# State products of two steps in 64 by 64 tiles, with the second step's heads swapped between the row halves

## The chip, the cores and the metric

The kernel runs on one core of one Trainium2 chip. The metric is device time in microseconds (us) of that core, the median of five runs. Engines are named as in the profile: PE (TensorE), PEld (its weight loads), DVE (VectorE), ACT (ScalarE), POOL (GpSimd), SP (the queue that issues most of the DMAs).

## The reference, cut to what matters

Decaying linear attention over 4 batches, 8 heads of 64 and 768 positions is followed by a feed-forward block with a sine gate.

```python
for b in range(nb):                                   # blocks of 64 positions
    intra = np.einsum('bhic,bhjc->bhij', qb, kb) * Dmask[None]
    intra = np.einsum('bhij,bhjd->bhid', intra, vb)
    inter = np.einsum('bhid,bhde->bhie', qb * lam_pow[None], kv_state)
    out[:, :, sl] = intra + inter
    kv_state = lam_block * kv_state + np.einsum('bhsd,bhse->bhde', kb * rev_pow, vb)
x = attn_out.transpose(0, 2, 1, 3).reshape(B * S, H * D)
h = x @ w_in                                          # 3072 x 512 @ 512 x 2048
s = np.sin(alpha * h)
g = h + s * s / (alpha + 1e-09)
out = g @ w_out                                       # 3072 x 2048 @ 2048 x 512
```

## The kernel before, in words

The 3072 rows are taken in 24 *steps* of 128 positions; a step is one block of 128 positions of one batch with its 8 heads. Steps come in pairs: an even and an odd step are the same block of two batches (`place`), so each batch has its own state and a pair shares nothing but buffers. Blocks are 128 long here (the reference's 64 are regrouped), and q and k are scaled by powers of lambda beforehand, so that the state is a plain running sum. Four steps make a *chunk* of 512 rows, and six chunks go through the feed-forward block.

Of one step s the orders name these pieces; the letter is the tag in the written orders, and the line that of the profile:

- `Lk`, `Lq`, `Lv`: loads, issued by SP (L392).
- `k`, `q`, `v`: scaling to bf16 (L507; L513 for the first 8 steps, L516 for the others) and the cast of v (L471), on POOL, DVE or ACT.
- `T` (L536, L539), for steps 0 to 7: 8 transposes of 128x128 by PE into a bank of PSUM and a copy `tc`; later steps are transposed by a DMA (`DT`, SP). The result is qkT: rows 0-63 hold the even head of each head pair, rows 64-127 the odd head.
- `S` (L554): scores of 8 heads, 8 matmuls that contract over 64 rows, give 128 keys x 128 queries, and go to two banks, one for each row half. `mask` (L559): two DVE products of 128x512.
- `P` (L570): product of q with the state, 4 matmuls of 128 rows x 128 columns. The state Zs is held as blocks of 128x128, one for each head pair, with zeros off the diagonal, so one matmul does both heads. P opens the bank (start).
- `I` (L577): masked scores times v, 8 matmuls of 128 rows and 64 output partitions, added to the same bank; then `x` (L471) copies the bank to xT.
- `Z` (L599), once per pair: 16 matmuls of 64 columns that add k'v to the state of both steps in the bank Z_ps; then `zs` (L471): two copies of 64x512, one per half of the rows, into Zs. The zeros are written once at the start (L454).
- The first block of a batch has no P; the last has no Z.

Of one chunk: `A` (L619), 16 products of 4 matmuls of 512 columns; `sin` (ACT, L624), `sq` (L629 on ACT, L630 on POOL or DVE), `g` (DVE, L632); `B` (L642), for each of its 4 steps 16 matmuls of 512 columns in four parts `B chunk.step.part`; `oc` copies it out (L471) and `st` stores it (L653). The very last step has its own function, `half_tile`: two groups `H0`, `H1` (L663) of 256 columns each, with copies `hc` and stores `hs`. `warm` (L676) are matmuls on zeros, in five groups of 14, 5, 2, 2 and 7 that fill PE before the first A.

Everything runs in an order that is written out by hand for each engine: the table `ORDER` (L19 to L85) has one list of tags for PE, DVE, ACT, POOL and SP. Semaphore waits are derived from what each piece reads and writes. `c0`, `c1`, ... are the constants in the order in which they are recorded; in PE's list, `c28` is the transpose of alpha (L463), which waits for alpha's DMA and is PE's first instruction. Seven banks `m_ps` go round by a list of free banks that follows PE's order. The weights come in 13 blocks `Lw` through a staging buffer, each cast in pieces `wc` by POOL, DVE or ACT.

Two stretches of PE's list, the start and the attention of steps 8 to 11, in chunk 1's output products:

```python
"c28 warm0 T1 T0 warm1 S1 warm2 S0 warm3 T3 T2 I1 S3 I0 Z0 S2 warm4 P3 P2 I3 I2 Z1 A0.2 A0.1 A0.0 "
...
"A1.13 A1.15 A1.8 A1.11 B1.1.0 B1.3.0 B1.3.1 B1.0.0 B1.1.1 B1.0.1 S8 S9 B1.1.2 B1.0.2 B1.0.3 P9 P8 I9 "
"I8 Z4 S11 S10 B1.3.2 B1.2.0 B1.3.3 P10 P11 I10 I11 B1.1.3 A2.9 A2.2 A2.4 A2.14 A2.1 A2.3 A2.13 "
```

Of the kernel before, what the change touches and what calls it, by code (L numbers as in the profile page):

```python
# [5 lines left out]
ALU = mybir.AluOpType  # L6
# [7 lines left out]
CHUNKS = [(0, 4), (4, 4), (8, 4), (12, 4), (16, 4), (20, 4)]  # L14
NG, NW, NPQ = 2, 6, 8
WARM = (
    14, 5, 2, 2, 7,
# [3 lines left out]
        "c28 warm0 T1 T0 warm1 S1 warm2 S0 warm3 T3 T2 I1 S3 I0 Z0 S2 warm4 P3 P2 I3 I2 Z1 A0.2 A0.1 A0.0 "  # L21
        "A0.7 A0.6 A0.4 A0.5 A0.3 A0.11 A0.8 A0.9 A0.10 A0.15 A0.14 A0.13 B0.1.0 A0.12 B0.0.0 B0.0.1 B0.3.0 "
        "B0.1.1 B0.3.1 B0.3.2 T4 B0.1.2 B0.2.0 B0.0.2 T5 S4 B0.0.3 B0.3.3 S5 P5 T6 B0.1.3 P4 T7 I4 S6 B0.2.1 "
        "Z2 I5 S7 B0.2.2 P6 P7 Z3 I6 I7 B0.2.3 A1.6 A1.10 A1.7 A1.5 A1.0 A1.9 A1.3 A1.1 A1.4 A1.2 A1.12 A1.14 "
        "A1.13 A1.15 A1.8 A1.11 B1.1.0 B1.3.0 B1.3.1 B1.0.0 B1.1.1 B1.0.1 S8 S9 B1.1.2 B1.0.2 B1.0.3 P9 P8 I9 "
        "I8 Z4 S11 S10 B1.3.2 B1.2.0 B1.3.3 P10 P11 I10 I11 B1.1.3 A2.9 A2.2 A2.4 A2.14 A2.1 A2.3 A2.13 "
        "B1.2.1 A2.12 A2.8 A2.7 A2.5 A2.10 A2.0 A2.6 B1.2.2 A2.11 B1.2.3 A2.15 B2.1.0 B2.1.1 S12 S13 B2.1.2 "
        "B2.2.0 B2.2.1 B2.1.3 B2.2.2 I13 Z6 I12 S15 S14 B2.3.0 B2.3.1 P14 B2.3.2 P15 I15 I14 Z7 S17 B2.2.3 "
        "A3.1 A3.0 B2.3.3 A3.10 A3.14 A3.2 A3.3 A3.13 B2.0.0 B2.0.1 A3.6 A3.12 A3.7 A3.8 A3.4 A3.5 B2.0.2 "
        "B2.0.3 A3.15 A3.9 A3.11 B3.0.0 B3.0.1 B3.3.0 B3.3.1 P17 I17 Z8 S16 S19 B3.3.2 B3.3.3 P16 I16 S18 "  # L30
        "B3.0.2 B3.0.3 P18 P19 I19 I18 Z9 B3.2.0 A4.0 A4.3 A4.5 A4.6 A4.10 A4.2 A4.4 A4.11 A4.14 B3.2.1 A4.7 "
        "A4.1 B3.2.2 B3.2.3 A4.15 A4.8 B3.1.0 B3.1.1 A4.13 A4.9 A4.12 B4.2.0 B3.1.2 B4.3.0 B4.3.1 B3.1.3 S20 "
        "S21 B4.2.1 B4.3.2 B4.3.3 P21 P20 Z10 I20 I21 S23 S22 B4.2.2 B4.2.3 B4.0.0 P23 P22 I22 I23 B4.0.1 "
        "A5.1 B4.0.2 A5.2 A5.7 A5.8 A5.6 B4.1.0 B4.0.3 B4.1.1 A5.0 A5.3 A5.12 A5.10 A5.4 A5.5 B4.1.2 A5.11 "
        "A5.9 B4.1.3 B5.1.0 A5.15 B5.2.0 A5.14 B5.2.1 A5.13 B5.1.1 B5.0.0 B5.0.1 B5.0.2 B5.1.2 B5.0.3 B5.1.3 "
        "B5.2.2 B5.2.3 H1 H0 "
    ),
    "DVE": (
        "c10 c11 c19 c25 c12 c3 c14 c15 c5 c16 c1 k0 k3 tc1 mask1.1 mask1.0 mask0.0 mask0.1 tc2 mask3.1 "
        "mask3.0 mask2.0 mask2.1 x0 x2 wc1.0 c31 wc1.6 sq0.1 g0.1 g0.2 g0.0 sq0.7 sq0.4 sq0.6 g0.7 g0.6 g0.4 "  # L40
        "g0.5 g0.3 g0.11 sq0.8 g0.8 g0.9 sq0.10 g0.10 wc2.10 g0.15 wc2.8 g0.14 q5 g0.13 g0.12 wc2.14 mask4.1 "
        "mask4.0 k7 mask5.0 mask5.1 tc6 oc1 tc7 mask6.0 mask6.1 mask7.1 mask7.0 x6 oc2 q9 q8 sq1.6 g1.6 "
        "sq1.10 g1.7 g1.10 sq1.9 zs3.1 g1.5 g1.0 g1.9 g1.3 g1.1 g1.4 sq1.2 g1.2 g1.12 sq1.14 g1.14 g1.13 "
        "g1.15 g1.11 g1.8 v8 mask8.0 mask9.0 mask8.1 mask9.1 q15 x8 mask11.0 mask10.1 mask11.1 mask10.0 x10 "
        "v13 oc7 sq2.9 k12 g2.9 g2.2 sq2.4 g2.14 g2.4 sq2.3 g2.1 g2.3 sq2.12 g2.13 g2.12 sq2.5 g2.8 g2.5 g2.7 "
        "g2.0 g2.6 g2.11 g2.10 oc6 mask12.0 v16 g2.15 mask13.1 v12 mask13.0 mask12.1 oc9 mask15.1 mask14.0 "
        "mask15.0 mask14.1 x15 v18 q19 mask17.0 oc10 q18 sq3.1 mask17.1 sq3.0 g3.0 g3.1 oc11 sq3.10 g3.14 "
        "g3.10 g3.2 g3.3 sq3.6 g3.13 g3.12 g3.6 g3.8 g3.7 g3.5 g3.4 sq3.15 g3.15 v19 oc8 g3.9 g3.11 mask16.0 "
        "mask16.1 mask19.1 zs8.1 mask18.0 mask19.0 mask18.1 q23 x19 oc12 g4.0 g4.3 g4.5 sq4.6 g4.10 g4.6 "
        "zs9.1 g4.4 g4.2 sq4.11 g4.11 g4.14 g4.1 oc14 g4.7 g4.8 g4.15 g4.13 g4.9 g4.12 mask21.1 mask20.0 "  # L50
        "mask21.0 mask20.1 x20 mask23.0 mask22.0 mask22.1 mask23.1 x22 g5.1 g5.2 sq5.6 oc16 g5.8 g5.7 g5.6 "
        "g5.3 g5.0 sq5.12 g5.12 g5.10 g5.4 g5.5 g5.9 g5.11 g5.14 g5.13 g5.15 oc22 hc1 "
    ),
    "ACT": (
        "lam c27 c0 c4 c17 c7 c29 c6 c18 tc0 c26 tc3 wc1.2 x1 zs0.0 zs0.1 v2 x3 sin0.2 sin0.1 sin0.0 sq0.2 "
        "sin0.7 sin0.6 sin0.4 wc1.8 sin0.5 sin0.3 sin0.11 sq0.3 sq0.11 sin0.8 sin0.9 wc2.2 sq0.9 sin0.10 "
        "wc2.6 sin0.15 sq0.15 sin0.13 sin0.14 sin0.12 sq0.14 zs1.1 sq0.12 tc4 wc2.12 tc5 zs1.0 oc0 oc3 v4 v5 "
        "x4 zs2.0 zs2.1 x5 x7 zs3.0 sin1.6 sin1.10 sin1.7 sq1.7 st0 sin1.5 sin1.9 sin1.0 sin1.3 sin1.1 sin1.4 "
        "sq1.4 sin1.12 sin1.2 sin1.13 sin1.15 sin1.14 sq1.15 sq1.13 sin1.11 v11 sin1.8 sq1.8 oc4 x9 zs4.1 "
        "zs4.0 st3 x11 oc5 st2 sin2.9 sin2.2 sq2.2 sin2.14 sin2.4 sq2.14 sin2.1 sin2.3 sq2.1 sin2.13 sin2.12 "  # L60
        "sq2.13 sin2.8 sin2.5 sin2.7 sq2.8 sin2.0 sin2.6 sin2.10 sin2.11 sq2.11 sq2.10 v15 sin2.15 sq2.15 x13 "
        "zs6.0 x12 zs6.1 st6 x14 zs7.0 sin3.1 sin3.0 sin3.10 sin3.14 sin3.2 sq3.2 sq3.14 sin3.13 sin3.3 "
        "sq3.13 sin3.6 sin3.12 st4 sin3.7 sin3.8 sin3.4 sq3.7 sin3.5 sq3.5 zs7.1 sin3.15 sin3.9 sin3.11 sq3.9 "
        "sq3.11 x17 x16 zs8.0 oc15 v23 x18 sin4.0 sin4.3 sin4.5 zs9.0 sq4.3 sin4.10 sin4.6 sq4.10 sin4.2 "
        "sin4.4 sq4.2 sin4.14 sin4.7 sin4.11 sin4.1 sq4.7 sq4.1 sin4.15 sin4.8 v20 sq4.8 sq4.15 sin4.13 "
        "sq4.13 st14 sin4.9 sin4.12 sq4.9 oc13 oc19 zs10.1 x21 zs10.0 oc18 x23 sin5.1 sq5.1 sin5.2 sin5.7 "
        "sin5.8 sin5.6 sq5.7 sq5.8 sin5.0 sin5.3 sq5.3 sq5.0 sin5.10 sin5.4 sin5.12 sq5.10 sin5.5 sq5.4 "
        "sin5.9 sin5.11 sq5.11 oc17 sin5.14 sq5.14 sin5.13 sin5.15 sq5.13 oc20 oc21 st21 hc0 hs0 "
    ),
    "POOL": (  # L70
        "c8 c23 c9 c20 c22 c13 c2 k1 q0 q2 c24 q1 k2 q3 c30 v1 v0 v3 wc1.4 sq0.0 wc1.10 wc1.14 sq0.5 wc1.12 "
        "wc2.0 q4 wc2.4 sq0.13 k4 k5 q6 k6 q7 v7 v6 k8 k9 sq1.5 sq1.0 sq1.3 sq1.1 q10 sq1.12 k10 k11 q11 "
        "sq1.11 v10 v9 c21 q12 k13 v17 q14 q13 k14 q17 sq2.7 sq2.0 sq2.6 k15 v14 k17 k16 k19 k18 q21 sq3.3 "
        "k21 sq3.12 sq3.8 sq3.4 q16 q20 k23 k22 v21 sq4.0 sq4.5 sq4.4 v22 sq4.14 q22 k20 sq4.12 sq5.2 sq5.5 "
        "sq5.9 sq5.15 "
    ),
    "SP": (
        "Lk1 Lq0 Lq2 Lq1 Lk3 Lk0 Lk2 Lq3 Lv1 Lv0 Lw1 Lv2 Lv3 Lw0 Lw2 Lw3 Lw4 Lw6 Lw5 Lq4 Lw8 Lw7 Lk4 Lw10 Lw9 "
        "Lk5 Lq5 Lw11 Lw12 Lq6 Lk6 Lk7 Lq7 Lv4 Lv5 Lv7 Lv6 Lq9 Lk8 Lq8 Lk9 Lv8 Lq10 Lv10 Lv11 Lk10 DT8 Lk11 "
        "Lq11 Lk13 Lq15 DT9 Lv9 Lk12 DT10 Lq12 DT11 Lv13 Lk16 st1 Lv15 Lq14 Lv17 Lq13 Lk15 Lq17 Lk14 Lv16 "  # L80
        "Lk17 Lv14 Lv23 st5 Lv12 DT12 Lq16 DT13 Lk19 DT14 Lq23 Lv20 DT15 Lq18 DT17 Lq19 Lv18 Lk20 Lv19 st7 "
        "Lk21 Lq21 Lk18 Lv21 DT19 st11 st10 Lq20 Lv22 DT18 st9 DT16 Lk23 st8 Lk22 DT21 Lq22 DT23 DT22 st15 "
        "st12 DT20 st13 st19 st16 st17 st18 st20 st22 hs1 "
# [153 lines left out]
def bass_lightning_attn__then__act_snake_kernel(  # L237
# [31 lines left out]
    with es:  # L269
# [18 lines left out]
        Zs = sb("Zs", [128, 2, HP, 128], BF16)  # L288
# [44 lines left out]


# [4 lines left out]
        for tag in in_pe_order:  # L339
# [14 lines left out]
            if a == "P":  # L354
                bank_of[tag] = free.pop(0)
                uses[bank_of[tag]].append((tag, ()))
                continue
            if a == "I" and f"P{rest}" in bank_of:
                i = bank_of[tag] = bank_of[f"P{rest}"]
                uses[i].append((tag, (f"x{rest}",)))  # L360
                free.append(i)
                continue
# [3 lines left out]
            i = bank_of[tag] = free.pop(0)  # L366
# [10 lines left out]

        def place(s):

            return 2 * (s // (2 * NB)) + s % 2, s // 2 % NB  # L380
# [13 lines left out]
        def consts():  # L394
# [50 lines left out]
            if NPQ:  # L445
# [5 lines left out]
                    out=bass.AP(maskP, 0, [[128, 128], [32, 4], [1, 32]]), in_=bass.AP(maskf, 0, [[128, 128], [32, 4], [1, 32]]), pattern=[[-1, 4], [-4, 32]],  # L451
                    compare_op=ALU.is_gt, fill=1.0, base=0, channel_multiplier=1),
                    reads=["maskf"], writes=["maskP"])
            rec("DVE", lambda e: e.memset(Zs[:, :, :, :], 0.0), writes=["Zs.0", "Zs.1"])  # L454
            rec("ACT", lambda e: e.activation(junk[:, :], maskf[:, 0:1], ACTF.Sin),
                reads=["maskf", "Lk", "Lq"] + (["L4.0", "L4.1"] if NPQ else []), writes=["junk"])

# [282 lines left out]
```

## Time and profile before

| | |
|---|---|
| median of five runs | 213.61 us (213.25 to 214.04) |
| the profiled execution | 213.47 us, of which the span is 211.6 us |
| PE | 202.6 us busy (96%), 1503 matmuls |
| DVE | 143.7 us (68%) |
| ACT | 127.5 us (60%) |
| POOL | 80.6 us (38%) |
| A, L619 | 384 matmuls, 86.5 us |
| B, L642 | 368 matmuls, 86.3 us |
| S, L554 | 192 matmuls, 8.5 us |
| I, L577 | 192 matmuls, 8.3 us |
| P, L570 | 80 matmuls, 6.6 us |
| Z, L599 | 160 matmuls, 4.2 us |

The span runs from the first to the last instruction of the profiled execution. The profile gives each matmul from its start to its end, and matmuls are pipelined: a mean of 379 ns for one L619 is a latency, and the busy time of the group is what it takes of PE (86.5 us for 384, 225 ns each). Where groups overlap at their seams, their busy times count the overlap twice; the chain of waits, which follows the work that ended last back to its start, does not. Its pieces are therefore used for prices. The granted clock of PE is 1.0 in the whole record of the clock.

### The profile page before, as it was taken

The page shows a single profiled execution, that of the slowest core. Times are in us where ns is not written, and L with a number is a line of the kernel's source. Part 1 is how long each engine was busy: PE and PEld are TensorE (multiplying, and loading weights), DVE is VectorE, ACT ScalarE, POOL GpSimd, SP SyncE. Part 2 cuts the span into 40 slices and gives each one's busy share as a digit, 9 for nine tenths or more (in the row PEclk, how much of TensorE's full clock was granted, in tenths as well). Part 3 has the DMA queues.
Part 4 walks back from the last instruction along what each step waited for, and adds up shares of the span by engine and source line. Part 5 has one row for each costly group of instructions (what it writes and reads, how often), then busy time and mean ns, then how long its engine had stood idle before and what let it go on. Part 6 is the DMA issues. An engine that isn't in the chain of part 4 may idle for free.

```text
span 211.6 us, 3791 instructions
## 1 busy us (share of the span) xinstructions
PE 202.6 (96%) x1503; PEld 101.8 (48%) x1503; DVE 143.7 (68%) x232; ACT 127.5 (60%) x211; POOL 80.6 (38%) x93
## 2 busy tenths in 40 slices
PE   0998999999999999999999999999999999999994
PEld 0365444556544465444455444564444464444453
DVE  4168799778799877897977678692975552656410
ACT  3057799675587623878344778446887155695520
POOL 2761574643449740548410457123441000103100
PEclk9999999999999999999999999999999999999999
DMA  5999999999999999999999992643053110101022
GB/s 150 258 264 344 366 355 343 346 229 226 208 225 209 203 260 250 255 241 217 162 246 272 239 262 43 160 91 62 0 149 99 53 50 3 48 2 65 34 98 104
DMA packets 94242, 38.02 MB, mean 180 GB/s; under 512 B 84352, under 2 KB 87696, under 8 KB 94224
## 3 DMA queue, kind: packets, MB, share of 16 engines
q1 hardware_dynamic: 92896, 35.79, 72.5%
q10 hardware_dynamic: 1328, 1.98, 2.7%
q8 instruction: 12, 0.20, 0.4%
q14 instruction: 6, 0.05, 0.1%
HBM read 27.28 MB, written 6.29 MB: 159 GB/s over the span
## 4 chain that ended last, share of the span: by engine, by line
PE 95%; DMA 2%; ACT 1%; DVE 0%; issue 0%; ACTq 0%
PE m_ps L619 39%; PE m_ps L642 38%; PE m_ps L676 4%; PE m_ps L554 3%; PE m_ps L577 3%; PE m_ps L570 2%; DMA alpha_r<-in_moe_alpha_dram 2%; PE m_ps L663 2%; PE Z_ps L599 1%; PE m_ps L539 1%; PE m_ps L536 1%; ACT qkT L471 0%; DVE xT L471 0%; ACTq L395 0%; ACT osb L471 0%
## 5 line engine op out<-in xcount | busy, mean ns | idle before, releaser
L619 PE MATMUL m_ps<-xT,w 128*128 128x512 bf16 x384 | 86.5, 379 | 0.5 <-DVE xT L471 0.5
L642 PE MATMUL m_ps<-w,gT 128*128 128x512 bf16 x368 | 86.3, 380 | 0.0
L632 DVE SCALAR_TENSOR_TENSOR gT<-u,r_sb,m_ps 128x512 bf16<-128x512 bf16 x96 | 67.4, 743 | 22.3 <-ACT u L629 14.5
L624 ACT ACTIVATE t<-m_ps,alpha_sb 128x512 bf16<-128x512 f32 x96 | 63.4, 686 | 23.8 <-PE m_ps L619 23.6
L619 PEld LDWEIGHTS m_ps<-xT,w 128*128 128x128 bf16 x384 | 37.5, 98 | 45.7 <-DVE xT L471 0.6
L642 PEld LDWEIGHTS m_ps<-w,gT 128*128 128x128 bf16 x368 | 34.5, 98 | 40.5
L630 POOL TENSOR_TENSOR u<-t 128x512 bf16<-128x512 bf16 x25 | 26.0, 1047 | 60.8 <-ACT t L624 60.7
L507 POOL TENSOR_TENSOR qk<-k,Lk 128x512 bf16<-128x512 f32 x20 | 22.1, 1110 | 31.5 <-DMA k<-in_k_dram 18.1
L629 ACT ACTIVATE u<-t 128x512 bf16<-128x512 bf16 x46 | 28.0, 629 | 0.5
L559 DVE TENSOR_TENSOR S_m<-m_ps,mask 128x512 bf16<-128x512 f32 x32 | 20.2, 683 | 6.9 <-PE m_ps L554 6.8
L471 ACT CAST xT<-m_ps 128x512 bf16<-128x512 f32 x15 | 8.8, 585 | 20.2 <-PE m_ps L577 20.2
L471 ACT COPY osb<-m_ps 128x512 f32<-128x512 f32 (+1 forms) x12 | 6.8, 566 | 21.4 <-PE m_ps L642 16.7
L630 DVE TENSOR_TENSOR u<-t 128x512 bf16<-128x512 bf16 x25 | 14.1, 567 | 6.7 <-ACT t L624 6.6
L471 DVE COPY osb<-m_ps 128x512 f32<-128x512 f32 (+1 forms) x13 | 8.7, 667 | 7.4 <-PE m_ps L642 5.6
L559 DVE TENSOR_TENSOR S_m<-m_ps,maskP 128x512 bf16<-128x512 f32 x16 | 10.1, 684 | 3.0 <-PE m_ps L554 3.0
L516 POOL TENSOR_TENSOR qk<-q,Lq 128x512 bf16<-128x512 f32 x10 | 10.9, 1102 | 2.9 <-DMA q<-in_q_dram 2.9
L471 POOL CAST v<-v 128x512 bf16<-128x512 f32 x11 | 6.7, 611 | 13.0 <-DMA v<-in_v_dram 13.0
L471 DVE CAST xT<-m_ps 128x512 bf16<-128x512 f32 x9 | 6.2, 691 | 7.1 <-PE m_ps L577 7.0
L471 ACT CAST Zs<-Z_ps 64x512 bf16<-64x512 f32 x17 | 9.8, 578 | 1.4 <-PE Z_ps L599 1.3
L471 ACT COPY qkT<-m_ps 128x1024 bf16<-128x1024 bf16 x4 | 4.0, 1012 | 9.7 <-PE m_ps L539 9.7
L676 PE MATMUL m_ps<-zeros,ident 128*128 128x512 bf16 x30 | 9.9, 482 | 0.0
L471 POOL CAST w<-wst 128x1024 bf16<-128x1024 f32 x6 | 6.7, 1125 | 6.2 <-DMA wst<-in_moe_w_in_dram 4.7
(61 smaller groups left out, 114.9 us busy)
## 6 DMA issues: line engine op xcount, KB each, us to landing
k<-in_k_dram SPq DMA_DIRECT2D x24, 256.0 KB, 5.2
q<-in_q_dram SPq DMA_DIRECT2D x24, 256.0 KB, 4.6
v<-in_v_dram SPq DMA_DIRECT2D x24, 256.0 KB, 4.7
wst<-in_moe_w_out_dram SPq DMA_DIRECT2D x8, 512.0 KB, 6.1
out_dram<-osb SPq DMA_DIRECT2D x16, 256.0 KB, 2.6
wst<-in_moe_w_in_dram SPq DMA_DIRECT2D x3, 1024.0 KB, 6.8
out_dram<-osb ACTq DMA_DIRECT2D x7, 256.0 KB, 3.5
wst<-in_moe_w_in_dram SPq DMA_DIRECT2D x2, 512.0 KB, 6.3
```

Of the source, the lines that this page charges most:

```text
L471: return e.copy(out_ap, in_ap) if name == "ACT" else e.tensor_copy(out_ap, in_ap)
L507: rec("POOL DVE", lambda e, _: e.tensor_tensor(k2[c], k32[r][:, :, :], Lk_b, ALU.mult), reads=[f"k32.{r}", "Lk"], writes=[f"k2.{c}"], tag= ...
L516: rec("POOL DVE", lambda e, _: e.tensor_tensor(q2[c], q32[r][:, :, :], Lq_b, ALU.mult), reads=[f"q32.{r}", "Lq"], writes=[f"q2.{c}"], tag= ...
L554: last = e.matmul(dst[h][:, jp, :], qkT[j][rows, 4 + jp, :], qT(s, rows, jp))
L559: rec("DVE", lambda e, h=h: e.tensor_tensor(S_m[j2][:, 4 * h:4 * h + 4, :], dst[h], mask_b, ALU.mult), reads=[f"S{s}", "maskP" if s < NPQ ...
L619: last = e.matmul(m_ps[i][:, 0:n], w1[:, kc, 128 * m:128 * (m + 1)], xT[x][:, kc, 0:n], start=(kc == 0), stop=(kc == NKC - 1))
L624: rec("ACT", lambda e: e.activation(t16[tt][:, 0:n], m_ps[i][:, 0:n], ACTF.Sin, scale=alpha_sb[:, m:m + 1]), reads=[f"A{c}.{m}", "alpha"], ...
L629: return e.activation(u16[tt][:, 0:n], t16[tt][:, 0:n], ACTF.Square)
L630: return e.tensor_tensor(u16[tt][:, 0:n], t16[tt][:, 0:n], t16[tt][:, 0:n], ALU.mult)
L632: rec("DVE", lambda e: e.scalar_tensor_tensor(out=gT[g][:, m, 0:n], in0=u16[tt][:, 0:n], scalar=r_sb[:, m:m + 1], in1=m_ps[i][:, 0:n], op0 ...
L642: last = e.matmul(m_ps[bank][:, :], gT[g][:, m, 128 * s4:128 * (s4 + 1)], w2[:, m, :], start=(m == 0), stop=(m == NM - 1))
L676: last = e.matmul(m_ps[bank_of[f"warm{i}"]][:, :], ident[:, :], zeros[:, :])
```

## The change

The state Zs loses its zeros: it is 128 rows x 2 steps x 4 head pairs x 64. The even step keeps the even head of a pair in rows 0-63 and the odd head in rows 64-127; the odd step has them swapped (`prep` writes its q and k so, and Z, S and the masks follow). P is now done once for a pair of steps, after both I: 16 matmuls of 64 rows x 64 output partitions x 128 columns, in turn through the four combinations of row half and output half. I opens the bank and P ends it, and both x copies of the pair wait for P. S has 16 matmuls of 64x64 in place of 8 of 64x128. `zs` is one copy of 128x512. The clearing of Zs goes (later constants have numbers lower by one). The last step is split at column 384 instead of 256. The warm-up has four groups, of 14, 3, 1 and 9 matmuls. All five orders are written anew: alpha's transpose (`c27`) stands behind S1, loads begin k1, k0, q1, q0, v1; DVE has 14 k products (4 before) and 35 squares (25), ACT 38 squares (46) and 13 stores (7), POOL 10 k products (20).

```diff
-    14, 5, 2, 2, 7,
+    14, 3, 1, 9,
...
-        "c28 warm0 T1 T0 warm1 S1 warm2 S0 warm3 T3 T2 I1 S3 I0 Z0 S2 warm4 P3 P2 I3 I2 Z1 A0.2 A0.1 A0.0 "
+        "warm0 T0 warm1 T1 S0 T2 warm2 S1 c27 T3 I0 Z0 S2 I1 S3 warm3 I3 I2 P1 Z1 A0.0 A0.1 A0.2 A0.3 A0.6 "
+        "A0.4 A0.5 A0.11 A0.8 A0.7 A0.10 A0.14 A0.12 A0.9 A0.15 B0.1.0 B0.3.0 B0.0.0 A0.13 B0.2.0 B0.0.1 "
...
+        "A1.14 B1.0.1 A1.13 B1.3.0 A1.12 B1.3.1 B1.3.2 S8 S9 B1.0.2 B1.3.3 B1.0.3 I9 Z4 I8 S11 P4 S10 B1.1.0 "
+        "B1.1.1 B1.1.2 I11 I10 P5 B1.1.3 A2.4 A2.3 A2.2 A2.11 A2.6 A2.13 A2.1 A2.9 A2.14 B1.2.0 A2.7 A2.5 "
...
-        Zs = sb("Zs", [128, 2, HP, 128], BF16)
+        Zs = sb("Zs", [128, 2, HP, D], BF16)
...
-            rec("DVE", lambda e: e.memset(Zs[:, :, :, :], 0.0), writes=["Zs.0", "Zs.1"])
...
+            o, sh = (D, -D) if s % 2 else (0, D)
+            own = lambda t: bass.AP(t, o, [[2 * H * D, 128], [2 * D, HP], [sh, 2], [1, D]])
+            of = lambda t: bass.AP(t, 0, [[H * D, 128], [2 * D, HP], [D, 2], [1, D]])
+            table = lambda t: bass.AP(t, n * H, [[NB * H, 128], [2, HP], [1, 2], [0, D]])
+            k_out = bass.AP(qk2[c], o + H * D, own(qk2[c]).ap)
+            rec("POOL DVE", lambda e, _: e.tensor_tensor(k_out, of(k32[r]), table(Lk), ALU.mult),
...
-                        last = e.matmul(dst[h][:, jp, :], qkT[j][rows, 4 + jp, :], qT(s, rows, jp))
+                        for i in range(2):
+                            keys = slice(64 * i, 64 * i + 64)
+                            last = e.matmul(dst[h][keys, jp, :], qkT[j][rows, 4 + jp, keys], qT(s, rows, jp))
...
-            def before_block(e):
-                for jp in range(HP):
-                    last = e.matmul(dst[:, jp, :], Zs[:, j, jp, :], qT(s, slice(0, 128), jp),
-                                    start=(jp == 0), stop=False, skip_group_check=True)
-                return last
...
+            def before_block(e):
+
+                for jp in range(HP):
+                    for two in range(2):
+                        for r in range(2):
+                            half, rows = 64 * (r ^ two), slice(64 * r, 64 * r + 64)
+                            last = e.matmul(
+                                dst[s - 1 + two][half:half + 64, jp, :], Zs[rows, two, jp, :],
+                                qT(s - 1 + two, rows, jp), start=False, stop=(jp == HP - 1), skip_group_check=True)
+                return last
             if n:
-                rec("PE", before_block, reads=[f"qkT.{jq}", "Zs.0", "Zs.1"], writes=[f"I{s}"], tag=f"P{s}")
+                rec("PE", before_block, reads=[f"qkT.{(s - 1) % NQ}", f"qkT.{jq}", "Zs"],
+                    writes=[f"I{s - 1}", f"I{s}"], tag=f"P{s // 2}")
...
+                                r = h ^ two
                                 last = e.matmul(
-                                    Z_ps[64 * h:64 * h + 64, two, jp, :], k2[cc][:, 2 * jp + h, :],
+                                    Z_ps[64 * r:64 * r + 64, two, jp, :], k2[cc][:, 2 * jp + r, :],
...
-                for h in range(2):
-                    rows, cols = slice(64 * h, 64 * h + 64), slice(64 * h, 64 * h + 64)
-                    rec("ACT DVE", lambda e, name, rows=rows, cols=cols: copy_of(
-                        e, name, Zs[rows, :, :, cols], Z_ps[rows, :, :, :]), reads=["Z"], writes=[f"Zs.{h}"],
-                        tag=f"zs{s // 2}.{h}")
+                rec("ACT DVE", lambda e, name: copy_of(e, name, Zs[:, :, :, :], Z_ps[:, :, :, :]), reads=["Z"],
+                    writes=["Zs"], tag=f"zs{s // 2}")
...
-            cs = slice(256 * half, 256 * half + 256)
+            c0, c1 = ((0, LAST), (LAST, DM))[part]
+            w = c1 - c0
```

Here `LAST` is 384. `grp_A` is rewritten so that a product could be done in two parts (`Aa`), but no order has such a tag, so it does what it did.

## The prediction

> **What bounds the kernel now.** I read the chain of waits first, because a 96% busy TensorE can still be a queue with holes. The end of its summary and its first stretch:
>
> ```profile
> PE 95%; DMA 2%; ACT 1%; DVE 0%; issue 0%; ACTq 0%
> PE m_ps L619 39%; PE m_ps L642 38%; PE m_ps L676 4%; PE m_ps L554 3%; PE m_ps L577 3%; PE m_ps L570 2%; DMA alpha_r<-in_moe_alpha_dram 2%; PE m_ps L663 2%; PE Z_ps L599 1%; PE m_ps L539 1%; PE m_ps L536 1%; ACT qkT L471 0%; DVE xT L471 0%; ACTq L395 0%; ACT osb L471 0%
> ```
>
> The reader is to see that the chain is TensorE itself: 5.3 us ahead of its first matmul, then 203.5 us of its own queue, then 2.8 us of tail. The waits of TensorE confirm it:
>
> ```profile
> PE Z_ps L463 <- DMA alpha_r<-in_moe_alpha_dram: 5.3, 1, 5.3
> PE m_ps L619 <- DVE xT L471: 0.5, 1, 0.5
> PE m_ps L554 <- ACT qkT L471: 0.4, 1, 0.4
> ```
>
> After the first feed-forward matmul (21.29 us) it never waits on another engine for long. So a change is worth what it takes out of TensorE's queue, plus what it moves at the two ends, less any new hole. Second, the chain in order of time gives the price of each piece without overlap. Columns: start, us, what.
>
> ```profile
> 44.58 0.22 PE m_ps L539 x4
> 44.80 0.33 PE m_ps L554 x8
> 45.13 1.83 PE m_ps L642 x8
> ...
> 53.15 0.45 PE m_ps L570 x8
> 53.60 0.37 PE Z_ps L599 x16
> 53.97 0.45 PE m_ps L577 x16
> 54.42 0.97 PE m_ps L642 x4
> ...
> 74.38 0.55 PE m_ps L554 x16
> ```
>
> L570 is P, the state product: 8 full matmuls of 128 columns in 0.45, 0.056 each; one after the other. L577 is I: 16 matmuls of 128 columns in 0.45, 0.028 each: two 128x64 column tiles run at once. L554 is S: 8 take 0.33 and 16 take 0.55, so 0.22 per step of 8 (two row tiles at once) and 0.11 once. Z's 16 matmuls of 64 columns take 0.25 to 0.37. Four L642 take 0.86 elsewhere and 0.97 here, behind I: again 0.11. That 0.11 is the price of a change of tile shape.
>
> **The change, part by part.** The sum is made on the profiled execution: 213.47 us, its span 211.6; the median of five runs is 213.61, 0.14 above.
>
> *1. State products.* Before: two steps x 4 matmuls = 0.45 per pair of steps. After: 16 matmuls of 64x64 for the pair, in an order that goes round all four tiles. If four run at once: 16/4 x 0.056 = 0.22; if two at a time, as I and S show: 16 x 0.028 = 0.45. Nine of the ten pairs stand behind the first feed-forward matmul (the tenth is hidden in the start). Bounds: 0 to -9 x 0.22 = -2.0.
>
> Here a rule speaks against the change. The Trainium skill's "TensorEngine Tiling (Array Packing)", "Restrictions and Gotchas", says that different row tiles go to different PSUM banks and cannot access one bank at the same time. In S before, the two row tiles write two banks; in the new P, rows 0-63 and rows 64-127 write one bank, in opposite halves of the partitions. By the rule, P runs two at a time, 0.45: no gain. The rows show each half of the question: I's two column tiles write one bank in opposite partition halves and overlap (0.028), S's two row tiles write the same partitions of two banks and overlap (0.028). What the new P adds is a row pair with a shared bank and no shared partition. I take it as nearest to I, where sharing a bank costs nothing: -2.0, and keep 0 as the other end.
>
> *2. Scores in 64 by 64 tiles.* 16 matmuls instead of 8 per step, each still 128 columns; the row halves keep their own banks, the key halves own partition halves. Four at once: 0.22, as now; two at once: 0.45. The same page ("Tile-to-Partition Mapping", "Restrictions") says column tiling switches fast weight load off. S was row-tiled only, so by the rule its weight loads slow down and may stop hiding: loads of column-tiled shapes are longer in the trace (L577 110 ns, L599 112, against 94 for L554), but Z puts 16 loads and 16 matmuls into 0.25 us, 16 ns a pair, so they overlap. Four tiles in 0.056 need 14 ns a pair. At Z's rate S costs 0.25 instead of 0.22. I take +0.015 per step for 20 steps: +0.3; bounds 0 and +4.6 (two at once).
>
> *3. Changes of tile shape.* Counting neighbours in the two written orders behind the first feed-forward matmul: 42 changes before, 48 after. P used to have the shape of the big matmuls and stood behind them without a change; now it has another shape than I and Z, which stand ahead of it. 6 x 0.11 = +0.6. Bounds: +0.3 (a change into or out of a small group may hide) to +0.9.
>
> *4. Copies of the state.* One 128x512 copy per pair in place of two of 64x512: ACT's took 578 ns each, DVE's 694. It removes 8 x 0.58 = 4.6 us from ACT and 1.4 from DVE; both lie beside TensorE (ACT is 60% busy). P waits for the copy, and the orders leave it 2.8 us or more between Z and the next P, against 1.5 or more before. Zero on the path; the removed clearing of Zs (0.49, DVE) lies before zeros is needed by lambda's landing: zero.
>
> *5. The start.* The first matmul no longer waits for alpha: warm-up can begin when zeros is written, which follows lnlam (lambda lands at 3.93): about 4.9 instead of 5.5; alpha's transpose now stands behind S1 at about 13.5, its data there by 8.7 (issued behind Lk at 4.7, 3.97 to landing). Loads are reordered: k1, k0, q1, q0 first. By the intervals of landing in the trace (0.75 per q, 1.1 per k or v), k2 lands at 11.75 and q3 at 12.5, v1 a step earlier than now. Followed by hand with the rows' durations (DVE k 0.69, q 0.89, copy 0.68, mask 0.62 to 0.68; POOL 1.04; ACT copy 1.01): T0 at 10.55, T2 at 12.5, T3 at 13.75, S3 at 15.7, masks of steps 2 and 3 finished at 18.2, P1 at 18.6, x copies at 19.75, first feed-forward matmul at 19.9 against 21.29. What is late next are weights: the fourth block lands at 25.38 in the trace, behind the same bytes, and the DMA row stands at 9 throughout; its two casts, both on POOL, end at 26.5 and 27.6. The eighth and ninth products need them and would start at 25.95 and 27.4: a hole of about 0.8. Net: 0.6 earlier. Bounds: 0 to -1.4.
>
> *6. Holes behind the start.* The last w_out blocks landed at 42.3 and 43.7, and their casts ended at 43.8 and 44.4; the changed order asks for them at about 44.0, the old one at 45.1: some 0.4. DVE gets 10 more k products and 10 more squares (0.93 and 0.57 each) and loses 4 output copies, 2 state copies: near +10 us, 143.7 to 154 of 210. In the stretch of the second chunk (first gate of chunk 1 to first of chunk 2) its written work sums to 26.3 us for 27.4 of TensorE's, against 25.4 for 28.6: fuller, and the masks of steps 8 and 9 have some 0.1 us of room. I take another 0.2. Bounds 0 to +1.5 together; I take +0.6.
>
> *7. The end.* The last tile goes 384 + 128 columns instead of 256 + 256: the same columns for TensorE (3.5 us), but the last copy shrinks: ACT 0.58 at 512 columns, 0.37 at 256, so 0.27 at 128; and half the bytes to store. -0.2; bounds 0 and -0.4. The first copy (0.48) hides under the second group (0.9). Tail issues moved to ACT (13 against 7) lie in its idle time.
>
> Sum: -2.0 + 0.3 + 0.6 + 0 - 0.6 + 0.6 - 0.2 = -1.3 of the span; from the median 213.6 that makes 212.3.
>
> **Rivals.** (a) *Forecast*, 212.3: four tiles at once, holes partly eat the start. Chance 0.50; its own range is 211.3 to 213.1 by the smaller bounds. (b) *No holes*: the start's 1.4 is kept and step 6 is 0: -2.0 + 0.3 + 0.6 - 1.4 - 0.2 = -2.7, 210.9. For it: the old order ran behind its start with hardly a hole; against it: the DMA row is full. Chance 0.17. (c) *The gain goes into waits*: P shares the bank badly (part of -2.0 missing), or DVE's fuller stretch makes TensorE wait 1 us more: 213.2 to 214.0, taken as 213.6. For it: DVE at 96% of one stretch. Against: DVE's operations overlap a little at their ends (two gates in 1.41 of chained time). Chance 0.16. (d) *Slower*: 64x64 tiles go two at a time, because of the bank or the weight loads. Then P gains nothing, S costs 0.22 more on 20 steps: -0 + 4.6 + 0.6 - 0.6 + 0.6 - 0.2 = +5.0, 218.6; if only half of it, 216. Its deciding point: with P and S both paying, a gain of 1.6 without S's term is gone over 20 x (d/0.056) x 0.22 + 9 x (d/0.056) x 0.22 = 1.6, at d = 0.014: four tiles in 0.070 instead of 0.056. For it: no row shows four tiles; the rule. Against: I and S each show their half. Chance 0.17. That the change doesn't do what it says would be P in two groups or Zs still padded; the diff excludes both.
>
> **Numbers.** 0.2% (0.4 us) is what a measurement of this kernel can tell from no change. Faster by more: nearly all of (a) and (b), a quarter of (c): 0.67. Within: the rest of (a), half of (c): 0.13. Slower: (d) and a quarter of (c): 0.20. The range leaves out the upper part of (d) and the far end of (b): 210.6 to 215.0.
>
> **What would show it.** P's groups of 16 in the chain at 0.22 to 0.33 with a change, against 0.45 or more; S at 0.22 to 0.25 per step; four L642 still at 0.97 behind a small group. The first feed-forward matmul near 20, and a wait on POOL's weight cast near 26. TensorE's waits on DVE staying under 1 us in all. If S takes 0.45 the forecast is wrong at step 2; if P does, at step 1; if TensorE shows waits over 1.5 us, at step 6.

## The result and the profile after

The changed kernel takes 212.98 us, the median of 43 runs (211.67 to 214.84), and the kernel before 213.78 in 80 runs beside them (212.98 to 214.94): a ratio of 0.9963 with a 95% interval of 0.9951 to 0.9975. Medians, ranges and ratios here and below leave out slow runs, of over 1.5% above the fastest of their kernel: one of the changed kernel (215.4), two of ten with the loops turned, and two of twelve in each of the two versions with transposes moved. The changed kernel is 0.8 us faster; forecast were 1.3. Its runs are spread more widely than those of before (over 3.2 us against 2.0), and that is the first thing to read: the profiled execution of the changed kernel, 214.18 us with a span of 212.4, is 1.2 us above its own median. A second profile of it, from the first experiment, is of an execution of 212.31 us with a span of 210.5. The two together show more than either.

The chain of waits of the first profile, summed by engine; before, it read PE 95%:

```profile
PE 58%; SPq 19%; DMA 13%; DVE 3%; POOL 2%; ACT 2%; issue 1%
```

TensorE's busy time is as it was (202.4 us, 95% of the span) and does not show the gain. What has changed is that the chain now leaves TensorE for stretches at a time and runs through SP's queue and *landings*, the arrivals of a DMA's data. The shares say how far back the chain goes, not what it costs: in the second profile they still read PE 77% only, with far smaller waits. TensorE's waits on other engines in the same profile (in all, times, longest):

```profile
PE m_ps L706 <- DVE sel L428: 4.6, 1, 4.6
PE Z_ps L622 <- POOL v L477: 1.3, 2, 1.1
PE m_ps L643 <- ACT xT L477: 0.5, 1, 0.5
PE m_ps L546 <- DVE qk L517: 0.4, 1, 0.4
PE m_ps L643 <- POOL w L477: 0.4, 1, 0.4
PE m_ps L584 <- POOL v L477: 0.2, 1, 0.2
```

The first line is the start and replaces 5.3 us of waiting for alpha. Those on a cast are new: Z (L622) and I (L584) wait for a cast of v, and a feed-forward product (L643) for a cast of weights. The pieces of the chain in the stretch that gave the prices of before, steps 8 to 11:

```profile
77.80 0.23 PE m_ps L584 x8
78.02 0.35 PE m_ps L566 x16
78.37 0.22 PE m_ps L598 x16
78.59 0.22 PE m_ps L566 x16
78.82 2.69 PE m_ps L670 x12
81.51 0.57 PE m_ps L584 x16
82.08 0.35 PE m_ps L598 x16
82.42 0.97 PE m_ps L670 x4
```

L598 is P: 16 matmuls of 128 columns in 0.22 us, 0.014 each, where its 8 full ones took 0.45. L566 is S: 0.22 for its 16. Both have four tiles running at once: the matmuls of P start in fours, within 10 ns of each other, every 56 ns. The price of a change of shape is where it was: S behind I 0.35 and P behind I 0.35, each 0.13 more; P directly behind S, or S behind P, nothing; four L670 behind P 0.97.

Cut at the first product of the first chunk, at that of the second chunk, and at the end of the last matmul, the three profiled executions read (us, differences of start times in the traces):

| stretch | before | changed, first profile | changed, second profile |
|---|---|---|---|
| up to the first product | 21.29 | 20.11 | 20.45 |
| to the second chunk's first product | 33.93 | 35.53 | 34.99 |
| to the end of the last matmul | 153.58 | 154.32 | 152.61 |
| behind it | 2.77 | 2.43 | 2.44 |

The start is 0.8 to 1.2 earlier, and the second chunk starts at 55.64 and 55.44, against 55.22: no earlier at all. Behind that, the second profile gains 1.0 and the first loses 0.7. The difference between the two is holes on TensorE. A hole is what lies between the starts of two matmuls beyond the pitch of their form (216 ns at 512 columns). Over 0.15 us, and beyond a change of shape, the first profile has 0.57 and 0.20 at 26 and 31 us (weights), 0.18 at 52 (inside a product, nothing shown that ends it), 0.33 at 53 (v7), 0.17 at 107 (between two steps' scores), 1.29 at 110 (v15) and 0.27 at 122 (most likely a bank, behind DVE), 3.0 in all; the second has 0.47 at 26, 0.42 at 52 (the same place) and 0.24 at 53, 1.1 in all. The kernel before has none behind its first product.

### The profile page after: what moved, and what is told of

Same layout as the page of the kernel before. It is cut to its first block, busy times and chain, and to the rows that moved or that the text cites. A ratio compares the mean times of both kernels' runs of the same rounds, so it can differ in the third digit from the quotient of the medians.

```text
span 212.4 us, 4308 instructions
## 1 busy us (share of the span) xinstructions
PE 202.4 (95%) x1772; PEld 98.0 (46%) x1772; DVE 147.5 (69%) x243; ACT 119.1 (56%) x197; POOL 72.0 (34%) x85
## 4 chain that ended last, share of the span: by engine, by line
PE 58%; SPq 19%; DMA 13%; DVE 3%; POOL 2%; ACT 2%; issue 1%
PE m_ps L670 26%; PE m_ps L643 26%; SPq L398 16%; DMA wst<-in_moe_w_in_dram 4%; DMA wst<-in_moe_w_out_dram 4%; DMA v<-in_v_dram 3%; DMA k<-in_k_dram 3%; PE m_ps L584 2%; SPq L539 2%; PE m_ps L693 2%; PE m_ps L566 2%; DVE gT L660 2%; SPq L496 1%; PE m_ps L598 1%; ACT t L652 1%
## 5 line engine op out<-in xcount | busy, mean ns | idle before, releaser
L643 PE MATMUL m_ps<-xT,w 128*128 128x512 bf16 x384 | 87.9, 379 | 1.0 <-ACT xT L477 0.5
L670 PE MATMUL m_ps<-w,gT 128*128 128x512 bf16 x368 | 87.3, 380 | 0.1
L643 PEld LDWEIGHTS m_ps<-xT,w 128*128 128x128 bf16 x384 | 36.8, 98 | 47.7 <-DVE gT L660 2.4
L670 PEld LDWEIGHTS m_ps<-w,gT 128*128 128x128 bf16 x368 | 34.5, 98 | 40.6 <-issue 0.3
L658 POOL TENSOR_TENSOR u<-t 128x512 bf16<-128x512 bf16 x23 | 24.0, 1044 | 79.6 <-ACT t L652 76.9
L477 ACT COPY osb<-m_ps 128x512 f32<-128x512 f32 (+2 forms) x17 | 9.5, 559 | 26.6 <-PE m_ps L670 19.4
L657 ACT ACTIVATE u<-t 128x512 bf16<-128x512 bf16 x38 | 23.4, 629 | 1.3 <-DVE osb L477 0.7
L526 POOL TENSOR_TENSOR qk<-q,Lq 128x512 bf16<-128x512 f32 x13 | 14.1, 1096 | 17.2 <-DMA q<-in_q_dram 17.2
L658 DVE TENSOR_TENSOR u<-t 128x512 bf16<-128x512 bf16 x35 | 16.9, 492 | 4.2 <-ACT t L652 4.1
L517 DVE TENSOR_TENSOR qk<-k,Lk 128x512 bf16<-128x512 f32 x14 | 9.8, 706 | 2.5 <-DMA k<-in_k_dram 2.5
L477 POOL CAST v<-v 128x512 bf16<-128x512 f32 x13 | 9.0, 689 | 7.6 <-DMA v<-in_v_dram 7.5
L517 POOL TENSOR_TENSOR qk<-k,Lk 128x512 bf16<-128x512 f32 x10 | 11.2, 1124 | 0.7 <-DMA k<-in_k_dram 0.7
L477 DVE COPY osb<-m_ps 128x512 f32<-128x512 f32 x8 | 5.5, 686 | 8.3 <-PE m_ps L670 8.3
L584 PE MATMUL m_ps<-S_m,v 128*64 128x128 bf16 x192 | 8.9, 223 | 0.2 <-POOL v L477 0.2
```

Source lines behind the costliest of these rows:

```text
L477: return e.copy(out_ap, in_ap) if name == "ACT" else e.tensor_copy(out_ap, in_ap)
L517: rec("POOL DVE", lambda e, _: e.tensor_tensor(k_out, of(k32[r]), table(Lk), ALU.mult), reads=[f"k32.{r}", "Lk"], writes=[f"k2.{c}"], tag= ...
L526: rec("POOL DVE", lambda e, _: e.tensor_tensor(own(qk2[c]), of(q32[r]), table(Lq), ALU.mult), reads=[f"q32.{r}", "Lq"], writes=[f"q2.{c}"] ...
L584: last = e.matmul(dst[s][64 * h:64 * h + 64, jp, :], v2[c][:, 2 * jp + h, :], S_m[j][:, 4 * (h ^ j) + jp, :], start=(jp == 0), stop=(not n ...
L643: last = e.matmul(m_ps[i][:, cols], w1[:, kc, 128 * m:128 * (m + 1)], xT[x][:, kc, cols], start=(kc == 0), stop=(kc == NKC - 1))
L657: return e.activation(u16[tt][:, 0:n], t16[tt][:, 0:n], ACTF.Square)
```

## The experiments

Theory W: the gain on TensorE's queue is there, and waits that end at landings take part of it, in other places from one execution to the next. Rival S: the gain is itself small, a fixed price. Theory F concerns the tiles: four at once cost what two do.

**The changed kernel again.**

> The changed kernel unchanged, a second profile beside the others of this call. Theory W (waits eat the gain): its holes on TensorE move from one execution to the next, because they end at landings; the wait of Z for the cast of v15 (1.29 us in the first profile) is again there, between 0.3 and 1.5 us, and the stretch up to the third chunk's first product again ends no earlier than in the kernel before. Rival S (a fixed price): every execution has the same holes within 0.1 us and the spread is elsewhere.

It measured 213.16 us, ratio 0.9971 (0.9944 to 0.9999). TensorE's waits in its profile:

```profile
...
PE m_ps L546 <- DVE qk L517: 1.3, 1, 1.3
PE m_ps L643 <- DVE xT L477: 0.5, 1, 0.5
PE m_ps L643 <- POOL w L477: 0.3, 1, 0.3
...
PE m_ps L584 <- POOL v L477: 0.2, 1, 0.2
```

The wait of Z for v15 is not there at all, so the expectation that it would be was wrong. So was the one on the third chunk, which starts 1.0 us earlier than before (83.12 against 84.11); it had done so in the first profile too (83.23). That the wait for v15 is absent speaks for W against a fixed price: same kernel, 1.29 us in one execution and none in another. The weights' hole and v7's are in both.

**The cast of v15 first.**

```diff
-        "k15 q13 sq2.9 k14 v12 q12 k16 q17 v15 q18 q21 k17 sq3.13 sq3.6 sq3.9 v16 sq3.4 v20 k18 v21 sq3.14 "
+        "k15 q13 sq2.9 k14 v12 q12 k16 v15 q17 q18 q21 k17 sq3.13 sq3.6 sq3.9 v16 sq3.4 v20 k18 v21 sq3.14 "
```

> On POOL the cast of v15 is put ahead of the product q17. Theory W: q17 waits for its load and holds up v15, whose data has landed long before; the hole of TensorE ahead of the state product of steps 14 and 15 (1.29 us in the profile of the changed kernel) goes, and the median falls by 0.4 to 1.2 us against the changed kernel, ratio to the kernel before 0.991 to 0.995. Rival (another wait takes its place: the load of v15 or the transposed q of step 15 is late too): the hole shrinks by less than half and the median stays within 0.3 us of the changed kernel.

It measured 214.42 us, ratio 1.0029 (0.9999 to 1.0059): slower than the changed kernel, not faster. Its twelve runs fall into two groups, six of 213.26 to 213.87 us and six of 214.96 to 216.16, with nothing between them; the profiled one, 214.96, is of the upper group. POOL's timeline in the first profile of the changed kernel (start, us, what; behind it the idle time ahead and who ended it) shows why the edit was tried:

```profile
96.50 1.22 POOL L517 TENSOR_TENSOR qk<-k,Lk 128x512 bf16<-128x512 f32 x1
109.22 1.04 POOL L526 TENSOR_TENSOR qk<-q,Lq 128x512 bf16<-128x512 f32 x1 [11.50 <-DMA q<-in_q_dram]
110.20 1.07 POOL L477 CAST v<-v 128x512 bf16<-128x512 f32 x1
```

q17 waited 11.5 us for its load with v15 queued behind it, though v15 had landed at 94.0. The second profile of the same kernel shows why the hole is missing there:

```profile
106.79 1.04 POOL L526 TENSOR_TENSOR qk<-q,Lq 128x512 bf16<-128x512 f32 x1 [9.14 <-DMA q<-in_q_dram]
107.78 0.61 POOL L477 CAST v<-v 128x512 bf16<-128x512 f32 x1
```

The load of q17 landed at 106.7 us instead of 109.2, so v15 was cast by 108.4, and TensorE asks for it at about 110. The other profiles with this order on POOL agree: the wait is there where q17 landed at 110.1 (the products in another order, the loops turned) and not where it landed at 108.1 (the scores in rows). So the time of one landing decides this hole. With the edit, POOL's timeline has v15 done in time and the same wait of q17 behind it:

```profile
99.98 0.80 POOL L477 CAST v<-v 128x512 bf16<-128x512 f32 x1
110.04 1.04 POOL L526 TENSOR_TENSOR qk<-q,Lq 128x512 bf16<-128x512 f32 x1 [9.26 <-DMA q<-in_q_dram]
```

The hole at v15 went, as expected. But the profile has another, ahead of the scores of step 9, at a place that runs before anything the edit touches; TensorE's timeline:

```profile
74.35 0.42 PE L566 MATMUL m_ps<-qkT 64*64 64x128 bf16 x16
76.27 0.42 PE L566 MATMUL m_ps<-qkT 64*64 64x128 bf16 x16 [1.50 <-DMA qkT<-qk]
```

The hole of 1.66 us between the two ends at the landing of step 9's transpose. The transposes of steps 8 and 9 landed at 73.7 and 76.2 here, at 71.4 and 73.5 in the changed kernel's first profile, and at 65.1 and 71.1 in the kernel before, where that of step 8 stood four loads earlier in SP's queue and was issued 4.2 us earlier. So one hole was closed and the median did not follow. The new hole is as wide as the distance between the two groups of runs (their medians are 1.6 us apart), but only a run of the upper group was profiled: that the lower group is without the hole is not shown.

**Another order of the first chunk's products.** The seven places 11 8 7 10 14 12 9 become 7 11 8 10 9 14 12, in all the orders.

```diff
-        "A0.4 A0.5 A0.11 A0.8 A0.7 A0.10 A0.14 A0.12 A0.9 A0.15 B0.1.0 B0.3.0 B0.0.0 A0.13 B0.2.0 B0.0.1 "
+        "A0.4 A0.5 A0.7 A0.11 A0.8 A0.10 A0.9 A0.14 A0.12 A0.15 B0.1.0 B0.3.0 B0.0.0 A0.13 B0.2.0 B0.0.1 "
```

> The products of the first chunk are put in another order (7, 11, 8, 10, 9, 14, 12 instead of 11, 8, 7, 10, 14, 12, 9 in those seven places), with their sines, squares and gates, so that those whose weights are there come first. Theory W (the stretch up to 54 us is bound by landings): the holes of 0.57 and 0.20 us at 26 and 31 us go, but the hole ahead of the state product of steps 6 and 7, which waits for v7 (landed at 53.0 us), grows by about as much; the median stays within 0.3 us of the changed kernel. Rival (the weights are the only gate): the median falls by 0.6 to 0.8 us.

It measured 213.64 us, ratio 1.0001 (0.9977 to 1.0026). The holes at 26 and 31 us went, and the profile has 0.63 at 33 us (a w_out cast on DVE) and 0.95 ahead of the state update of steps 4 and 5 instead (the cast of v5, on ACT); v15's is there again, with 1.05. This is the slowest of the twelve runs (215.18 us). The second chunk starts at 56.2 us. Taking out the weights' wait did not bring the second chunk forward in that execution: the next landing held it. There W's mechanism held, though at v5 rather than v7, and the median is 0.5 to 0.7 above the changed kernel's, where it was expected within 0.3.

**Scores in tiles of 64 rows by 128 columns.**

```diff
-                        for i in range(2):
-                            keys = slice(64 * i, 64 * i + 64)
-                            last = e.matmul(dst[h][keys, jp, :], qkT[j][rows, 4 + jp, keys], qT(s, rows, jp))
+                        last = e.matmul(dst[h][:, jp, :], qkT[j][rows, 4 + jp, :], qT(s, rows, jp))
```

> The changed kernel with scores in tiles of 64 rows by 128 columns as before, 8 matmuls per step; the rest is as changed. Theory F (four tiles at once cost what two do): a step of scores takes 0.22 us in both forms; the only difference is four more changes of tile shape behind the first feed-forward product (52 instead of 48), 0.4 us: the median rises by 0.1 to 0.5 us against the changed kernel. Rival (weight loads of 64 by 64 tiles cost 0.03 us a step and more): the median falls by 0.3 us or more.

It measured 212.63 us, ratio 0.9952 (0.9928 to 0.9977), against 0.9971 (0.9944 to 0.9999) for the changed kernel beside it: the intervals overlap almost wholly. S took 8.5 us in all (192 matmuls), against 8.8 and 9.0 for the 384. The scores' new form has no gain of its own; the expected loss of 0.1 to 0.5 did not show either.

**The kernel before with 64 by 64 scores.** The same edit the other way round, in the kernel before.

> The kernel before with nothing changed but the scores, in 16 matmuls of 64 by 64 instead of 8 of 64 by 128. Theory F: a step takes 0.22 us in either form and the number of changes of tile shape is the same (42), so the median stays within 0.3 us. Rival L (loads of column-tiled weights no longer hide): 0.03 to 0.06 us per step of 20, 0.6 to 1.2 us slower. Rival T (two tiles at a time): 4.6 us slower.

It measured 213.75 us, ratio 0.9999 (0.9978 to 1.0020): no difference. S took 8.7 us for 384 matmuls, against 8.5 for 192. This settles step 2: loads of column-tiled weights (106 ns each for L566, against 94 before) still hide.

**The state product's loops turned.**

```diff
-                for jp in range(HP):
-                    for two in range(2):
+                for two in range(2):
+                    for jp in range(HP):
                         for r in range(2):
```

> The changed kernel with the loops of the state product turned, so that eight matmuls alternate between rows 0-63 into partitions 0-63 and rows 64-127 into partitions 64-127 of one bank, and then eight between the two other tiles. Theory F: a row pair that shares a bank but no partition overlaps as other pairs do, so P takes 0.45 us for a pair of steps instead of 0.22, and the median rises by about 2.0 us at most, less where a hole behind it absorbs it (1.0 to 2.2 us). Rival R (the rule of one bank): the two cannot overlap, P takes 0.90 and the median rises by 4 to 6 us. Rival N: the order does not matter, P stays at 0.22.

It measured 214.20 us, ratio 1.0005 (0.9971 to 1.0039). The chain:

```profile
79.19 0.26 PE m_ps L598 x16
...
82.93 0.37 PE m_ps L598 x16
```

P takes 0.26 and 0.37, against 0.22 and 0.35: neither 0.45 nor 0.90, so F and R were both wrong on this order, and N was right to 0.04 us. In the trace of the first of these, four matmuls start within 19 ns and all 16 within 0.21 us. The records do not name the tile, but at 0.056 us for each matmul the two tiles of the first eight can have started only two of the four: the others must be of the second eight, ahead of their turn, on the tiles that are free. So P's part is at most 9 x 0.04 = 0.4 us. The rest of the 1.2 above the changed kernel's 212.98 is in other places: this profile, of an execution of 215.31 us, has 0.9 of wait for a transpose at 74 us and 1.2 for v15.

**Lighter loads, in both kernels.** q, k and v are loaded as contiguous rows of 2 KB from other places of their tensors: the same bytes and the same work on other data, so the output is not the reference's.

```diff
+            a = bass.AP(src.tensor, s * BL * H * D, [[H * D, 128], [1, H * D]])
+            d = bass.AP(dst[r], 0, [[H * D, 128], [1, H * D]])
```

> The kernel before with k, q and v loaded as contiguous rows of 2 KB (the same bytes from other places of the tensors, so the products are of other data; the work of all engines stays). Theory W: before had hardly a hole on TensorE behind its start, so lighter transfers change little: within 1 us of the kernel before, all of it ahead of the first feed-forward product. Rival: the kernel before is itself bound by its transfers and falls by over 1.5 us.

> The changed kernel with the same lighter loads (contiguous rows of 2 KB, the same bytes from other places). Theory W (the gain on TensorE is there, and waits for landings take it): the holes at the weights' casts, at v7, at the transposes of steps 8 and 9 and at v15 shrink or go, the second chunk starts 1 to 2 us earlier than before, and this kernel is 1.8 to 2.8 us faster than the kernel before with the same loads. Rival S (the gain on TensorE is itself small): the two differ by 0.8 us, as with the loads as they were.

The kernel before measured 214.29 us so, ratio 1.0025 (1.0003 to 1.0047); the changed kernel 211.89, ratio 0.9911 (0.9876 to 0.9945, from four runs). DMA queue q1 went from 74.0% of the engines' span to 54.4% in the changed kernel. Its waits, and below them one of the kernel before:

```profile
...
PE m_ps L638 <- DVE xT L472: 0.7, 1, 0.7
PE m_ps L541 <- DVE qk L512: 0.3, 1, 0.3
```

```profile
PE m_ps L614 <- DVE osb L466: 1.0, 1, 1.0
```

No wait for a cast of v, a cast of weights or a transpose is left in the changed kernel (both lines lie at or ahead of the first product; left out are the wait of the start and, where records of matmuls are missing, short waits for nothing). The same change of loads made the changed kernel 1.1 us faster (0.9963 to 0.9911, intervals just apart, the second of four runs only, and no run of the changed kernel with its own loads stands beside them) and the kernel before 0.5 slower, which is W and not S. The two differ by 2.4 us, inside the expected 1.8 to 2.8. But in its profile, the slowest of its ten runs, the kernel before waits 0.5 us longer for alpha, starts its first product at 21.89 instead of 21.29, and has a new wait of 1.0 for an output copy at 86 us, so its part of the 2.4 may not be the change's. The 211.9 of the changed kernel is also what its fastest runs with the loads as they were reach (211.67): the lighter loads seem to take away its slower runs (211.71 to 212.82). One expectation failed: the second chunk starts at 55.1 us, 0.1 earlier than before and not 1 to 2. There, 0.68 us lie inside one product, ahead of the fourth matmul of `B0.3.2`, the third part of step 3's block, at 52 us, with no wait on another engine shown. The same gap, in the same place, is 0.18 and 0.42 in the two profiles of the changed kernel and 0.31 with v15 first, and it is in neither that of before nor that of the scores in rows. What makes it is open.

**v15 and three transposes earlier.** On top of v15 ahead of q17, SP has DT8 ahead of Lv10, and DT9 and DT10 ahead of Lq14.

> The changed kernel with two places of the orders moved: on POOL the cast of v15 ahead of the product q17, and on SP the transposes of steps 8, 9 and 10 one to three loads earlier. Theory W: the holes ahead of the scores of steps 8 and 9 (1.66 us in one profile) and of the state product of steps 14 and 15 (1.29 in another) go, and only those of the first 55 us stay; median 0.4 to 1.0 us below the changed kernel, ratio to the kernel before 0.991 to 0.995. Rival (holes move on to the next landing): within 0.4 us of the changed kernel or above it, with other holes of over 0.3 us behind 55 us.

It measured 213.10 us (212.22 to 214.43), ratio 0.9981 (0.9956 to 1.0006). The transpose of step 8 landed at 65.8 us, and in the profiled execution (span 210.4) TensorE waited for no transpose and no v:

```profile
...
PE m_ps L546 <- DVE qk L517: 0.9, 1, 0.9
PE m_ps L643 <- DVE xT L477: 0.7, 1, 0.7
PE m_ps L643 <- POOL w L477: 0.2, 1, 0.2
```

The holes are absent, but this execution, of 212.23 us, is one of the two fastest of its twelve, and the changed kernel's second profile, as fast (212.31), has neither of these waits either. So it does not show that the edit removed them, and the median stayed where it was. On the median the rival held.

**The same with the scores in rows.**

> As the kernel with v15 and three transposes earlier, and scores in tiles of 64 rows by 128 columns as before. Theory F: within 0.4 us of it. If 64 by 64 scores cost something that the chain does not show, it is faster by more; it is also tried as the best version: ratio to the kernel before 0.990 to 0.996.

It measured 213.38 us, ratio 0.9980 (0.9952 to 1.0007): no difference to the kernel with 64 by 64 scores, and no better version. Its profile, of an execution of 215.58 us, shows what no other one does: TensorE at half of its clock. The rows of its page (40 slices of 5.3 us, in tenths):

```profile
PE   1969999999999699999999999999999999999995
...
PEclk9988999999999999999999999999999999999999
```

The record of the clock has it at one half from 14.3 to 17.7 us. In the 3.4 us ahead of that, TensorE was busy for 1.64, against 2.12 and 2.98 between the same times in the two profiles of the changed kernel and 3.40 in the kernel before; all three have a mean clock of 1.0. The first feed-forward product starts at 21.78, against 20.54 in the run above. Half the clock for 3.4 of the 206 us that the record covers makes a mean of 0.992 (an estimate), and a mean of 0.991 or 0.992 stands in 4 of the 43 runs of the changed kernel, with a median of 214.3 us against 212.9 for the other 39, and in two of the upper group with v15 first. In the 83 runs of the kernel before that stand beside these experiments it is never under 0.998. So a part of the changed kernel's spread comes from its start. The cause is probably the thinner warm-up (27 matmuls in four groups, against 30 in five), but that is not shown: one profile has the drop, and no run has a fuller warm-up.

**The last tile in equal halves.**

```diff
-LAST = 384
+LAST = 256
```

> The changed kernel with the last tile split 256 + 256 again, both copies still on ACT. If the shorter tail (2.43 us from TensorE's last matmul to the end, against 2.77 before) comes from the smaller last copy and store, it is 2.6 to 2.8 us here; if it comes from elsewhere, it stays at 2.4 to 2.5.

A single run: from the end of the last matmul to the end of the span 2.65 us, against 2.43 with 384 and 2.77 before. The other profiles of kernels with 384 have 2.43 to 2.50. So some 0.2 us of the shorter tail is the smaller last copy and store; the other 0.1 stays with the rest of the edit.

## Why the prediction was right, step by step

The mechanism was right: TensorE's queue got shorter by the state products and the start, and waits behind the start took more than half of that back. The size was right in part by luck, since the 0.3 us set down for the scores did not appear and the holes were larger than forecast, mostly in other places than those named.

- *Step 1, state products:* right in kind and size. P is 0.22 us per pair of steps. The rule of the Trainium skill's "TensorEngine Tiling (Array Packing)", "Restrictions and Gotchas", that different row tiles cannot be in one bank at the same time, does not show in the time: the new P has both row halves writing one bank, and its matmuls start in fours within 10 ns, every 56 ns. The two row halves write opposite halves of the partitions here; no run has them on the same ones.
- *Step 2, scores:* +0.3 was too much. Two experiments, one on each kernel, measured nothing.
- *Step 3, changes of shape:* the price of 0.11 stood (0.13 in places). Together with step 1, behind the second chunk's first product: seven pairs and four more changes, -7 x 0.22 + 4 x 0.11 = -1.1; the second profile, which has no hole of over 0.15 us there, measured 152.61 - 153.58 = -1.0.
- *Step 4, copies of the state:* zero on the path, as predicted; no profile shows a wait of P for Zs.
- *Step 5, the start:* predicted 19.9 for the first product, measured 20.11 and 20.45. The wait that was named at the eighth product, for a cast of weights, came where it was put (0.57 and 0.47). The ninth has none; the first profile has 0.20 at the thirteenth. Together that is 0.8 and 0.5 against 0.8 predicted.
- *Step 6, holes behind the start:* the mis-sized term, and only partly in the places named. Predicted were 0.4 for the last w_out blocks and 0.2 for DVE. The first profile of the changed kernel has 0.33 for v7, 1.29 for v15 and 0.27 at 122 us, 1.9 in all; the second 0.24 for v7, and both have the gap at 52 us that no wait explains (0.18 and 0.42). v15 behind q17 on POOL, and the transposes behind four more loads on SP, are queues that the written orders show and the prediction did not follow up. Waits at the w_out casts do appear, but in other executions (0.63 in the kernel with another order of products). DVE was set too high: its busy time went to 147.5 us, not 154, since a k product took 0.71 us there instead of 0.93 and a square 0.49 instead of 0.57.
- *Step 7, the end:* -0.34 instead of -0.2.

With the measured parts the median can be made up backwards: steps 1 to 3 are -9 x 0.22 + 6 x 0.11 = -1.3 for all nine pairs, the start -0.8 to -1.2, the end -0.3, in all -2.4 to -2.8; the result is -0.8; so holes take some 1.6 to 2.0 us of the median execution, against 0.8 + 0.6 predicted. That last figure is a difference, not a measurement; it lies between the holes of the two profiles, 1.1 and 3.0. The second profile's execution, 212.31 us, is the forecast (a) almost to the figure. Rival (b), 210.9 without holes, was reached by no run (the lowest is 211.67). The first profile, 214.18, has the size of rival (c) but not its cause: its largest hole ends at POOL's cast of v15, not at DVE. Rival (d) is excluded by the 0.22.

What stays open is why one load lands up to 2.4 us later in one execution than in another, and how the spread of 3 us divides between such landings and the clock at the start; what the gap at 52 us waits for; and whether kernels a place or two apart in their orders truly differ. Nor does any run have the new orders with the old state products, so what each is worth is read from the pieces of the chain and not tested apart. The version with v15 first, 214.42, and the changed kernel, 213.16 beside it, have intervals that meet at 0.9999. No experiment tells whether the difference is in the order of POOL or in the runs.

## What to carry to other kernels

Where one engine's queue is the whole time, work taken out of it is worth its price only as far as the next landing: ask, for each stretch, how much later than its data each piece ran, since that slack is all that can be gained there. Here 0.8 to 1.2 us at the start and about 1.3 in the products came to 0.8 in all. A queue that is worked off in order passes one late load on to what stands behind it (v15, landed at 94.0 us, was cast at 110.2 behind q17), so put pieces whose data is there ahead of pieces whose data is not; and judge a fix of one such wait by many runs, because a profile shows only the execution it was taken from.

## What was not expected of the hardware

TensorE does not need the four tiles to take turns in the program: eight matmuls on two tiles followed by eight on the other two took 0.26 us, against 0.22 with the four in turn, where two tiles at a time would have taken 0.45. And matmuls of 64 by 64 cost no more per step than those of 64 by 128 (0.22 us for 16 as for 8), with twice as many weight loads.
